# Moving one load within a period, and scaling the last outputs on one engine

## The chip, the cores and the metric

The kernel runs on one core of a Trainium2 chip. A core has five engines that run their own instruction streams and wait for each other by semaphores: TensorE (PE in the profile; its weight loads are listed apart as PEld), VectorE (DVE), ScalarE (ACT), GpSimd (POOL) and SyncE (SP), which here does nothing but issue DMAs. "SPq" and "ACTq" are the DMA-issuing queues of SyncE and ScalarE. The metric is the device time of one execution in microseconds (us); lower is better.

## The reference, cut to what matters

A gated linear attention over 4 batches, 8 heads, 768 tokens and 48 dimensions a head, followed by a two-layer block on the 3072 tokens (384 to 1024 to 384) with a SoLU activation and a layer norm between its two products:

```python
for t in range(S):                                   # S = 768
    state = alpha[:, :, t, :, None] * state + np.einsum('bhd,bhe->bhde', k[:, :, t], v[:, :, t])
    y[:, :, t] = np.einsum('bhd,bhde->bhe', q[:, :, t], state)
x = y.transpose(0, 2, 1, 3).reshape(B * S, H * D)    # (3072, 384)
h = x @ w_in                                         # (3072, 1024)
e = np.exp(h - h_max)
solu = h * e / (np.sum(e, axis=-1, keepdims=True) + 1e-09)
ln = (solu - mu) / np.sqrt(var + 1e-06) * g_ln
out = ln @ w_out                                     # (3072, 384)
```

`alpha`, the decay, is between 0.8 and 1.0.

## The kernel before

The 768 tokens are cut into G = 6 blocks of 128, and a block holds all four batches at once. For a block, attention is done in closed form: running products of alpha forwards and backwards (two families of scans on VectorE) scale the queries and keys, TensorE forms the scores, VectorE masks them, and TensorE reads out the old state (`read_state`) and the masked scores times v (`read_values`, 128 matmuls). The two-layer block follows: `up` makes 8 pieces of h (6 matmuls of 512 columns each) and their SoLU parts, `down` makes the output of one batch's 128 tokens in two halves (8 matmuls each), and `finish` scales it by the inverse deviation and stores it.

The work is overlapped by blocks. In period g (from 1 to 5) the up and down products of block g run in eight steps, and the attention of block g + 1 is woven into the same steps. The order is written out by hand: the instructions of each engine run in the order in which the code issues them, and no scheduler moves them. Two tables, `usual` and `first` (line 814 on), say what `attend` does in which step: `head` ahead of the step's up product, `behind` after it, `middle` and `tail` around the down product. `first` holds for period 1, `usual` for the others. Attention has nothing to do in period 5.

Three input buffers matter here, each with room for one block: `an` (alpha), `kn` and `qn`. They are filled by `load` (lines 137 to 143), which issues four DMAs of 192 KB from SyncE's queue, one for each batch. SyncE issues strictly in order, and a DMA waits there until its buffer has been read. For block a:

- "states v keys", step 0: the state is brought up to date, `load_v` fetches v, the keys are transposed and scaled, and k of block a + 1 is loaded.
- "on2 on0 on1", step 1: the forward scans.
- "lasts firsts", step 2: the queries are transposed and scaled, and q of block a + 1 is loaded.
- "alpha", step 6 (step 7 in period 1): `alpha_T` transposes alpha of block a + 1 out of `an` on VectorE, `alpha_over` tests its range on ScalarE (two passes over `an`), and `an` is loaded with alpha of block a + 2 if there is one.
- "back", step 7: the backward scans of block a + 1.

In steps 6 and 7 TensorE reads out the state and the values of block a. Alpha of blocks 0 to 3 is loaded by the opening code (line 800 for block 3); the step "alpha" loads blocks 4 (in period 1) and 5 (in period 2).

Stores also go through SyncE's queue, from the end of `finish` (line 534): a period has four of them. Behind the loop come the down products of the last block, all but their first half, and its four `finish` calls, which take another path (lines 510 to 517): the 128 x 384 result in PSUM is scaled by `r` into `o_sb` in two parts, columns 0 to 127 on VectorE and 128 to 383 on ScalarE, and stored from ScalarE's own queue.

Of the kernel before, what the change touches and what calls it, by code (L numbers as in the profile page):

```python
# [13 lines left out]
AF = mybir.ActivationFunctionType  # L14
ALU = mybir.AluOpType
AX = mybir.AxisListType
P = 128
# [15 lines left out]
def fast_path(ctx, tc, q, k, v, alpha, moe_w_in, moe_w_out, moe_g_ln, out):  # L33
# [12 lines left out]
    nc = tc.nc  # L46
    B, H, S, D = q.shape
    NTOK, DM = out.shape
    DFF = moe_w_in.shape[1]
    G = S // P  # L50
# [49 lines left out]
    an = const.tile([P, H, TQ, D], FP, name="an")  # L100
# [36 lines left out]
    def load(src, dst, g):  # L137
        t = slice(g * P, (g + 1) * P)
        for b in range(B):
            nc.sync.dma_start(  # L140
                out=dst[32 * b : 32 * b + 32].rearrange("t h u d -> t h (u d)"),
                in_=src[b, :, t, :].rearrange("h (t u) d -> t h (u d)", u=TQ),
            )
# [31 lines left out]
    def load_v(g):  # L175
        t = slice(g * P, (g + 1) * P)
        for dst, src in ((first_of, slice(0, E0)), (last_of, slice(E0, D))):
            for i in range(2):
                nc.sync.dma_start(
                    out=vn.rearrange("p b (h i) d -> p i (b h) d", i=2)[:, i, :, dst[i]],  # L180
                    in_=v[:, i::2, t, src].rearrange("b h p d -> p (b h) d"),
                )
# [11 lines left out]
    def firsts(src, dst):  # L194
        nc.vector.transpose(out=dst.rearrange("p h (t u) -> p h u t", u=TQ), in_=src[:, :, :, 0:E0])  # L195

    def lasts(src, dst):
        nc.vector.transpose(
            out=dst.rearrange("p j (i t u) -> p u j i t", u=TQ, i=2),
            in_=src[:, :, :, E0:D].rearrange("p (j i) u d -> p u j i d", i=2),  # L200
        )

    def alpha_T(g):
        nc.gpsimd.memset(aT[:, :, 0:1], 0.0)
        firsts(an, aT[:, 0:H, 1:SW])
        lasts(an, aT[:, H:NB, 1:SW])
# [20 lines left out]
    def scan_on(g, i):  # L227
        part = slice(NP * i, NP * i + NP)
        s = seed[i % 2]
        if i == 2:  # L230
            nc.vector.tensor_copy(out=fend[:, g], in_=h4[:, :, 1])

        least = small.tile([P, NP, 1], FP, name="least")
        nc.vector.tensor_scalar(out=least, in0=h4[:, part, 1:2], scalar1=LEAST, scalar2=None, op0=ALU.max)  # L234
        nc.vector.reciprocal(out=s[:, :, 0:1], in_=least)
        scan(aT[:, part], aT[:, part], s, False)

    def keys_T(g):
        firsts(kn, kT[:, 0:H])
        lasts(kn, kT[:, H:NB])  # L240

    def keys(g):
        for part in (slice(0, H), slice(H, NB)):
            nc.gpsimd.tensor_tensor(out=kT[:, part], in0=kT[:, part], in1=hk[:, part], op=ALU.mult)  # L244

    def apart():
        for i in range(2):
            nc.scalar.mul(
                out=qv[:, H : 2 * H].rearrange("p (j i) t -> p j i t", i=2)[:, :, i], in_=qe, mul=parity[:, i : i + 1]
            )  # L250

    def queries(i):
        part = slice(NP * i, NP * i + NP)
        q = qe if i == 2 else qv[:, part]
        nc.gpsimd.tensor_tensor(out=q, in0=q, in1=aT[:, part, 1:SW], op=ALU.mult)

    def decay(g):

        if g == 0:
            return  # L260
        for i in range(2):
            for rows, d in ((0, h4[:, i:H:2, 1:2]), (H, h4[:, H:NB, 1:2])):
                s = state[:, rows + i : rows + H : 2, all_of[i]]
                nc.gpsimd.tensor_tensor(out=s, in0=s, in1=d.to_broadcast([P, NP, D]), op=ALU.mult)
            nc.gpsimd.tensor_scalar(
                out=ends_state[:, :, i], in0=state[:, H + i : 2 * H : 2, last_of[i]], scalar1=parity[:, i : i + 1],
                scalar2=None, op0=ALU.mult,
            )
# [21 lines left out]
    def masked(half, batches=range(B)):  # L290
        a = masks[half]
        for b in batches:
            nc.vector.tensor_tensor(  # L293
                out=sT[:, b, half * NP : half * NP + NP], in0=a[b], in1=mask[:, None, :].to_broadcast([P, NP, P]),
                op=ALU.mult,
            )

    def keys_back(g, t=None):
        t = t or banks("tp", [NP, P], 3)
        for j in range(NB):  # L300
            nc.tensor.transpose(out=t[j // NP][:, j % NP], in_=kT[:, j], identity=ident)
        for i in range(3):
            nc.scalar.copy(out=kg[:, NP * i : NP * i + NP], in_=t[i])
# [201 lines left out]
    def finish(n):  # L505
        g, b = divmod(n, B)
        d = st[n]
        s, o = sums[:, n], d["o"][:, 0:DM]
        t0 = b * S + g * P
        if g == G - 1:  # L510
            o_sb = work.tile([P, DM], FP, name="o_sb")
            r = gr[g]["r"][:, b : b + 1]
            nc.vector.tensor_scalar(out=o_sb[:, 0:P], in0=o[:, 0:P], scalar1=r, scalar2=None, op0=ALU.mult)  # L513
            nc.scalar.activation(out=o_sb[:, P:DM], in_=o[:, P:DM], func=AF.Copy, scale=r)  # L514
            nc.scalar.dma_start(out=out[t0 : t0 + P, :], in_=o_sb)
            d.clear()
            return
        nc.vector.tensor_copy(out=s[:, 0:1], in_=d["o"][:, DM : DM + 1])
        t = small.tile([P, 1], FP, name="t")
        nc.vector.scalar_tensor_tensor(  # L520
            out=t, in0=s[:, 0:1], scalar=-1.0 / DFF, in1=s[:, 0:1], op0=ALU.mult, op1=ALU.mult
        )
        nc.vector.tensor_tensor(out=s[:, 3:4], in0=t, in1=gr[g]["s"][:, b : b + 1], op=ALU.add)  # L523
        if g == 0:

            o = work.tile([P, DM], FP, name="o_mean")
            nc.vector.scalar_tensor_tensor(
                out=o, in0=mean_sb, scalar=s[:, 0:1], in1=d["o"][:, 0:DM], op0=ALU.mult, op1=ALU.add
            )
        r = small.tile([P, 1], FP, name="r")  # L530
        nc.gpsimd.tensor_tensor(out=r, in0=s[:, 3:4], in1=mhalf, op=ALU.pow)  # L531
        o_sb = work.tile([P, DM], FP, name="o_sb")
        nc.scalar.activation(out=o_sb, in_=o, func=AF.Copy, scale=r)
        nc.sync.dma_start(out=out[t0 : t0 + P, :], in_=o_sb)
        d.clear()
# [154 lines left out]
    for i in (2, 0, 1):  # L690
        if i == 1:
# [3 lines left out]
            out=qe if i == 2 else qv[:, part], in0=t[i], in1=aT[:, part, 1:SW], op=ALU.mult  # L695
# [105 lines left out]
    for i in range(3):  # L801
# [11 lines left out]

    usual = dict(
        head={4: "keys_back", 5: "masked0", 6: "masked1"},
        behind={0: "states v keys", 1: "on2 on0 on1", 2: "lasts firsts", 3: "apart", 5: "decay", 6: "alpha", 7: "back"},
        tail={4: "scores0", 5: "scores1", 6: "begin read0 read1"},
        middle={7: "read2 read3 values"},
    )
# [2 lines left out]
        behind={0: "states v", 1: "on1", 2: "lasts firsts", 3: "apart", 5: "decay", 7: "alpha back"},  # L822
# [4 lines left out]
    def attend(a, what):  # L827

        more = a + 1 < G
        if what == "v":  # L830
            load_v(a)
        elif what == "keys":
            keys_T(a)
            keys(a)
            if more:
                load(k, kn, a + 1)
        elif what[:2] == "on":
            scan_on(a, int(what[2]))
        elif what == "lasts":
            lasts(qn, qe)  # L840
            queries(2)
        elif what == "firsts":
            firsts(qn, qv[:, 0:H])
            queries(0)
            queries(1)
            if more:
                load(q, qn, a + 1)
        elif what == "apart":
            apart()
        elif what == "decay":  # L850
            decay(a)
        elif what == "keys_back" and more:
            keys_back(a)
        elif what[:6] == "scores":
            scores(a, int(what[6]))
        elif what[:6] == "masked":
            masked(int(what[6]))
        elif what == "alpha" and more:
            alpha_T(a + 1)
            alpha_over(a + 1)  # L860
            if a + 2 < G:
                load(alpha, an, a + 2)
        elif what == "back" and more:
            for i in range(3):
                scan_back(a + 1, i)
        elif what == "begin":
            read_begin()
        elif what[:4] == "read":
            read_state(int(what[4]))
        elif what == "values":  # L870
            read_values(a)
        elif what == "states":
            next_state(a - 1)
# [57 lines left out]
    def compare(out, x, bound, op):  # L931
# [6 lines left out]
        out=chunks[:, :, 2], in0=sums[:, :, 2], scalar=0.25, in1=sums[:, :, 3], op0=ALU.mult, op1=ALU.is_le  # L938
# [6 lines left out]
    else:  # L945
# [9 lines left out]
        out=bad, in0=all_ok[0:1, 0:1], scalar1=float(P * ends[-1]), scalar2=None, op0=ALU.is_lt  # L955
# [451 lines left out]
```

## Time and profile before

| What | Value |
|---|---|
| Runs of the kernel before | 393.21, 398.35, 390.92, 398.58, 398.03 us |
| Their median | 398.03 us |
| The profiled execution | 393.18 us |
| Its span, from first to last instruction | 391.1 us |
| Mean granted clock of TensorE | 0.989 |
| Bytes moved by DMA | 30.79 MB |
| Alpha loads by `load` | 20 DMAs of 192 KB, 4.2 us to landing (median) |
| The two alpha loads of the step "alpha" | issued at 150.71 and 201.14 us |
| Stores of the last block | at 374.01, 376.56, 382.06 and 387.25 us |

The periods can be found in the trace by the first up product of each: period 1 starts at 112.5 us, period 2 at 153.6, period 3 at 212.2, period 4 at 269.3 and period 5 at 324.4. Busy time is a share of the span; a window's row gives its length, the busy time of each engine in it with the number of instructions, the granted clock of TensorE as a share of full speed, and the busy share of the DMA engines (which can come out a little over 1). In a timeline, the brackets at a line's end say how long the engine had been idle before it and what ended that.

### The profile page before, as it was taken

How to read it: one execution, taken by the hardware profiler on the slowest of the kernel's cores; microseconds unless marked ns; L12 is line 12 of the kernel's file. 1: busy time of each engine (PE TensorE's matmuls, PEld its weight loads, DVE VectorE, ACT ScalarE, POOL GpSimd, SP SyncE). 2: the span in 40 equal slices, each digit the busy share in tenths (PEclk: the TensorE clock that was granted, in tenths of full speed). 3: DMA queues.
4: the chain of work that ended last, by engine and by line, in shares of the span. 5: the costliest groups of instructions: out<-in, count | busy, mean ns of one | idle time of the engine just before them, and what ended most of it. 6: DMA issues, size and time to landing. Idle time of an engine off the chain costs nothing. (4 is left out here: it accounts for less than half of the span.)

```text
span 391.1 us, 10613 instructions
## 1 busy us (share of the span) xinstructions
PE 371.7 (95%) x4661; PEld 224.6 (57%) x4661; DVE 252.0 (64%) x421; ACT 143.6 (37%) x252; POOL 125.2 (32%) x135
## 2 busy tenths in 40 slices
PE   8798999788999999999998999999999999999995
PEld 8685345456665556656565656566555575555552
DVE  0989888996987767793754793755895511444420
ACT  2527774553424425225152225153223231333100
POOL 4020000041032992436412436412535620333210
PEclk9989999999899999999999999999999999999998
DMA  9975989303446303734030734000600000000011
GB/s 184 198 187 166 224 273 163 84 20 94 107 108 83 82 4 82 114 70 101 22 77 29 111 73 102 22 3 22 93 10 22 22 23 2 20 21 21 22 44 47
DMA packets 86567, 30.79 MB, mean 79 GB/s; under 512 B 68072, under 2 KB 84720, under 8 KB 86512
## 3 DMA queue, kind: packets, MB, share of 16 engines
q1 hardware_dynamic: 85488, 29.11, 34.8%
q10 hardware_dynamic: 1024, 0.92, 0.7%
q8 instruction: 38, 0.62, 0.7%
q14 instruction: 17, 0.14, 0.1%
HBM read 25.30 MB, written 4.72 MB: 77 GB/s over the span
## 5 line engine op out<-in xcount | busy, mean ns | idle before, releaser
L500 PE MATMUL o<-w_out,room 128*128 128x385 f32 x384 | 135.3, 496 | 1.1 <-DVE least L234 1.0
L389 PE MATMUL h<-x,w_in 128*128 128x512 f32 x288 | 132.2, 598 | 1.2 <-DVE g_col L619 1.2
L500 PEld LDWEIGHTS o<-w_out,room 128*128 128x128 f32 x384 | 72.0, 191 | 58.3 <-issue 15.9
L389 PEld LDWEIGHTS h<-x,w_in 128*128 128x128 f32 x288 | 53.0, 189 | 59.9 <-issue 48.7
L404 DVE TENSOR_TENSOR room<-h,e 128x512 f32<-128x512 f32 x40 | 27.7, 692 | 84.3 <-ACT e L403 84.1
L403 ACT ACTIVATE e<-h 128x512 f32<-128x512 f32 x40 | 23.9, 598 | 105.3 <-PE h L389 105.3
L531 POOL TENSOR_TENSOR r<-sums,mhalf 128x1 f32<-128x1 f32 x20 | 14.3, 715 | 138.7 <-DVE sums L523 138.7
L420 POOL TENSOR_TENSOR p<-p,e 128x512 f32<-128x512 f32 x30 | 41.7, 1390 | 15.7 <-ACT e L403 15.7
L405 ACT ACTIVATE u<-room 128x512 f32<-128x512 f32 x40 | 25.2, 631 | 42.3 <-DVE room L404 42.3
L293 DVE TENSOR_TENSOR sT<-a,mask 128x512 f32<-128x512 f32 x44 | 27.3, 682 | 9.9 <-PE a L282 9.9
L282 PE MATMUL a<-qv,kT 32*128 32x128 f32 x704 | 27.5, 288 | 4.5 <-DVE least L234 2.1
L282 PEld LDWEIGHTS a<-qv,kT 32*128 32x128 f32 x704 | 24.1, 194 | 12.0 <-issue 4.2
L220 DVE TENSOR_TENSOR_SCAN hT<-aT,unit 128x516 f32<-128x516 f32 x18 | 23.0, 1328 | 8.9 <-ACT aT L678 8.8
L244 POOL TENSOR_TENSOR kT<-kT,hT 128x1024 f32<-128x1024 f32 (+1 forms) x8 | 13.3, 1684 | 44.3 <-DVE kT L195 44.3
L420 DVE TENSOR_TENSOR p<-p,u 128x512 f32<-128x512 f32 x30 | 23.1, 771 | 6.5 <-ACT u L405 6.5
L314 PE MATMUL y<-sT,vn 128*32 128x128 f32 x768 | 23.6, 274 | 2.6 <-issue 2.0
L314 PEld LDWEIGHTS y<-sT,vn 128*32 128x32 f32 x768 | 20.9, 110 | 4.8 <-issue 3.9
L220 DVE TENSOR_TENSOR_SCAN aT<-aT,seed 128x516 f32<-128x516 f32 x18 | 23.0, 1278 | 0.6
L212 ACT ACTIVATE sq<-an,mone 128x1536 uint8<-128x1536 f32 x12 | 18.8, 1569 | 0.2
L314 PE MATMUL y<-qv,state 32*32 32x128 f32 x960 | 16.8, 277 | 1.0 <-DVE sT L293 0.9
L314 PEld LDWEIGHTS y<-qv,state 32*32 32x32 f32 x960 | 12.1, 103 | 7.8 <-issue 5.4
L351 ACT COPY x<-y 128x384 f32<-128x384 f32 x24 | 10.8, 481 | 15.5 <-PE y L314 15.4
(142 smaller groups left out, 379.4 us busy)
## 6 DMA issues: line engine op xcount, KB each, us to landing
an<-in_alpha_dram SPq DMA_DIRECT2D x20, 192.0 KB, 4.2
out_dram<-o_sb SPq DMA_DIRECT2D x20, 192.0 KB, 1.9
room<-in_moe_w_out_dram SPq DMA_DIRECT2D x8, 384.0 KB, 4.6
kn<-in_k_dram SPq DMA_DIRECT2D x16, 192.0 KB, 4.0
qn<-in_q_dram SPq DMA_DIRECT2D x16, 192.0 KB, 4.1
vn<-in_v_dram SPq DMA_DIRECT2D x10, 256.0 KB, 4.1
room<-in_moe_w_in_dram SPq DMA_DIRECT2D x16, 128.0 KB, 3.9
kn<-in_k_dram SPq DMA_DIRECT2D x4, 384.0 KB, 5.8
```

The costliest lines, as they stand in the source:

```text
L212: nc.scalar.activation(out=sq, in_=x, func=AF.Relu, scale=sign, bias=mone, accum_out=over[:, g, i : i + 1])
L220: nc.vector.tensor_tensor_scan(out=o, data0=a, data1=s, initial=1.0, op0=ALU.mult, op1=ALU.add)
L282: nc.tensor.matmul(a[b][:, i], lhsT=kT[quarter(b), kb], rhs=qv[quarter(b), qb], start=kb == h, stop=kb != h, tile_position=(32 * b, 0), sk ...
L293: nc.vector.tensor_tensor(out=sT[:, b, half * NP : half * NP + NP], in0=a[b], in1=mask[:, None, :].to_broadcast([P, NP, P]), op=ALU.mult,)
L314: nc.tensor.matmul(y_bank(b)[quarter(r), a], lhsT=lhsT, rhs=rhs, start=(b, r) not in begun, stop=stop, tile_position=(row, 32 * r), skip_g ...
L389: nc.tensor.matmul(h, lhsT=w_in[:, a, f * P : (f + 1) * P], rhs=d["x"][:, a].rearrange("p b t -> p (b t)"), start=(a == 0), stop=(a == KC ...
L403: nc.scalar.activation(out=e, in_=h, func=AF.Exp)
L404: nc.vector.tensor_tensor(out=u, in0=h, in1=e, op=ALU.mult)
L405: nc.scalar.activation(out=u2, in_=u, func=AF.Square)
L420: eng.tensor_tensor(out=p, in0=d[0][i] if f == 1 else p, in1=d[f][i], op=ALU.add)
L500: nc.tensor.matmul(d["o"][:, 0 : DM + 1], lhsT=u_of(g, f)[:, b * P : b * P + P], rhs=w_out[:, f], start=(f == 0), stop=(f == FC - 1), skip ...
L531: nc.gpsimd.tensor_tensor(out=r, in0=s[:, 3:4], in1=mhalf, op=ALU.pow)
```

## The change

Two edits. The load of the next alpha leaves the step "alpha" and becomes a step of its own, "load", in front of the forward scans of step 1 of the table `usual`. There it loads alpha of block a + 1, where the old place loaded that of block a + 2 one period earlier. The table `first` has no such step, so alpha of block 4 is loaded in period 2 and that of block 5 in period 3. In `finish`, the last block's scaling is one ScalarE instruction over all 384 columns.

```diff
         if g == G - 1:
             o_sb = work.tile([P, DM], FP, name="o_sb")
             r = gr[g]["r"][:, b : b + 1]
-            nc.vector.tensor_scalar(out=o_sb[:, 0:P], in0=o[:, 0:P], scalar1=r, scalar2=None, op0=ALU.mult)
-            nc.scalar.activation(out=o_sb[:, P:DM], in_=o[:, P:DM], func=AF.Copy, scale=r)
+            nc.scalar.activation(out=o_sb, in_=o, func=AF.Copy, scale=r)
             nc.scalar.dma_start(out=out[t0 : t0 + P, :], in_=o_sb)
...
     usual = dict(
         head={4: "keys_back", 5: "masked0", 6: "masked1"},
-        behind={0: "states v keys", 1: "on2 on0 on1", 2: "lasts firsts", 3: "apart", 5: "decay", 6: "alpha", 7: "back"},
+        behind={0: "states v keys", 1: "load on2 on0 on1", 2: "lasts firsts", 3: "apart", 5: "decay", 6: "alpha", 7: "back"},
...
         elif what == "alpha" and more:
             alpha_T(a + 1)
             alpha_over(a + 1)
-            if a + 2 < G:
-                load(alpha, an, a + 2)
+        elif what == "load" and more:
+            load(alpha, an, a + 1)
         elif what == "back" and more:
```

## The prediction

> **What bounds the kernel now.** I read the page's head first, then TensorE's waits, the order of time around the loads that move, the same passage of every period side by side, SyncE's queue, and the chain that ended last.
>
> The page:
> ```profile
> span 391.1 us, 10613 instructions
> PE 371.7 (95%) x4661; PEld 224.6 (57%) x4661; DVE 252.0 (64%) x421; ACT 143.6 (37%) x252; POOL 125.2 (32%) x135
> ```
> TensorE has work for 371.7 of 391.1 us. From about 110 us on its matmuls follow each other almost without a hole, so a change counts only if it takes time out of TensorE's row or out of the tail behind its last matmul. In TensorE's own waits (total, times, longest) the largest late item with no engine as its cause is:
> ```profile
> PE y L314 <- issue: 2.0, 2, 1.2
> ```
> "issue" means that no wait shown by the profile held it. The timeline places the longer one, in the second period:
> ```profile
> 201.14 1.82 SPq L140 DMA_DIRECT2D an<-in_alpha_dram  x4
> ...
> 204.31 2.81 PE L314 MATMUL y<-sT,vn 128*32 128x128 f32 x93
> ...
> 208.32 1.28 PE L314 MATMUL y<-sT,vn 128*32 128x128 f32 x35 [1.19 <-issue]
> ```
> An alpha load is issued at 201.14, and TensorE stops at 207.13 amid the 128 matmuls of read_values. The same 128 matmuls of every attention block, by windows (length, TensorE busy, granted clock, DMA share, GB/s):
> ```profile
> 104.92:109.77 4.85, 4.04 (x134) 1.00 0.64 135
> 146.69:150.85 4.16, 4.02 (x134) 1.00 0.02 4
> 204.31:209.53 5.22, 4.03 (x134) 1.00 0.38 98
> 262.99:266.62 3.63, 3.63 (x133) 1.00 0.06 20
> 318.11:321.74 3.63, 3.63 (x133) 1.00 0.16 59
> ```
> The clock is full in all five. The two dearest, 4.85 and 5.22 us, are the two with an alpha load in flight (issued at 103.13 and 201.14); without one it is 4.16 once and 3.63 twice.
>
> SyncE's queue between two periods:
> ```profile
> 158.27 4.59 SPq L179 DMA_DIRECT2D vn<-in_v_dram  x4
> 162.96 2.61 SPq L140 DMA_DIRECT2D kn<-in_k_dram  x4
> 166.73 0.37 SPq L534 DMA_DIRECT2D out_dram<-o_sb  x1
> 175.32 1.79 SPq L140 DMA_DIRECT2D qn<-in_q_dram  x4
> ```
> Last, the chain of waits at the end, and the nearest row for an undivided scaling, that of the earlier blocks (shortest, median and longest in ns):
> ```profile
> 386.37 0.35 DVE o_sb L513
> 386.72 0.02 issue
> 386.74 0.47 ACT o_sb L514
> ```
> ```profile
> L533 ACT ACTIVATE o_sb<-o,r x16: 580/580/582, 166.1 to 367.0; 128x384 f32<-128x384 f32 x16
> ```
> The two halves of the last scaling run one after the other: 0.35 + 0.02 + 0.47 = 0.84 us.
>
> **The change, part by part.** *The loads.* Neither bytes nor DMAs change. Alpha for block 3 still comes from line 800; those for blocks 4 and 5 (two loads of four DMAs) move. One was issued at 150.71, after period 1's reading; the other at 201.14, inside period 2's.
>
> The first is worth nothing where it was. The 7.29 us behind it (150.85 to 158.14) hold the same matmuls as 209.53 to 216.82 and 266.62 to 273.91, which have no load and also take 7.29 us. The second is worth what its passage costs over a clean one: 5.22 - 3.63 = 1.59 us. At the least, if the 4.16 us of period 1 is what such a passage costs anyway, it is 5.22 - 4.16 = 1.06 us. I take 1.59, since periods 3 and 4 both show 3.63.
>
> Why would a load stop TensorE without any wait? My reading is instruction supply. The page's queue table has 38 instruction packets of 0.62 MB on q8, some 16 KB each; 9322 TensorE instructions (4661 matmuls and as many weight loads) over 38 is about 245 to a packet, if that queue is TensorE's (an estimate). From 202.90 to 207.13 TensorE ran 190 matmuls and 189 weight loads, 379 instructions or one and a half packets, while the data engines were 0.68 busy. [...] I go with the rows: two of two passages with a load have a gap.
>
> At the new place, step 1 of the next period, each load stands in SyncE's queue behind v, k and the store at 166.73 (225.33 a period later), and ahead of the q load. It waits for nothing: the readers of the buffer, two transposes on VectorE and two range tests on ScalarE, ended by 150.7 and 201.1. Four issues take 1.8 us, so SyncE is free again at about 168.9, and q cannot be issued before 175.32 and 234.00 (it waits for VectorE's transposes of the old q). Even four issues at the longest seen for alpha, 1.84 us, end at 174.5. The store that stood behind the old load, at 206.92, followed its scaling at once and gains nothing. Alpha lands at worst 6.2 us after issue (its longest landing), near 175, and is read at 197.10: 22 us of cover. If that cover were gone, the transposes (2.09 + 1.11 us) and the three scans after them would be late and the next block's keys and scores with them. POOL issues no load.
>
> The collision at the new place: v and k hold the data engines at 1.0 to 1.2 from 160 to 168 and 0.59 from 168 to 170, so alpha lengthens a backlog of some 10 us by about 4. From 167.10 to 172.27 TensorE starts 15 matmuls and 14 weight loads, 29 instructions against the 379 after which it ran dry. I take 0. TensorE is unbroken there now, so nothing can be gained; the upper bound is 1.59 us for each of the two loads (the row of the old place).
>
> *The scaling.* Each of the four last chunks loses 0.35 us on VectorE and costs ScalarE 0.58 instead of 0.47. The first three lie beside TensorE, which is continuous from 370.12 to 386.26; they end about 0.26 us earlier or on time. The last one is the path: 0.84 becomes 0.58, so -0.26 us. ScalarE starts as promptly as VectorE: its Exp at 353.89 began 0.09 us after the matmul's end, VectorE's scaling at 386.36 0.10 after. Bounds: -0.26, and 0 if the wait costs ScalarE the rest.
>
> **The sum:** -1.59 - 0.26 = -1.85 us. The profiled execution took 393.18 us (span 391.1, 2.1 around it); with the change 391.3. The five runs lie in two groups, 390.92 and 393.21, and 398.03 to 398.58; the profiled execution belongs to the lower, the median, 398.03, to the upper. Nothing in one trace says what parts them, so I take the sum off the median: 396.2.
>
> **The rivals.**
> *Only the tail counts.* The gap is not the load's. [...] Then -0.26: 392.9 by the profiled execution, 397.8 by the median.
>
> *The upper group is the stall itself.* If in the longer runs such a passage stops TensorE by several microseconds more (the groups are about 5 us apart), then taking it away moves the runs to the lower group: 390.92 - 1.85 = 389.1 to 393.21 - 1.85 = 391.4. For it: nothing else late in TensorE's row is loose. Against: the opening has more waits, which stay, and has one such passage too (4.85 us).
>
> *Slower: TensorE runs dry at the new place.* v, k and alpha in one row starve the instruction supply in step 1 of both periods. Price: at most the 4.2 us of an alpha landing each, plus a clock that has to recover. The windows from 98 to 104 us show 0.76, 0.50 and 0.89 granted behind gaps of 1.48 and 0.85 us, and a down pass there took 4.55 instead of 2.86 us, 1.69 more. [...] 2 x (4.2 + 1.69) - 1.85 = +9.9 us: 408 by the median. It decides once TensorE needs more than it holds within the transfer; 29 instructions against 379 speak against it.
>
> That the change does something else than it says I leave at nothing: in either version there is one load for each block before its transposes.
>
> **How the numbers follow.** Forecast 0.52, tail only 0.22, upper group gone 0.18, dry at the new place 0.08. The predicted time is the forecast's, 396.2. The range goes from 389.0 (the third case's low end) to 399.0 (no gain, at the highest run shown). About 2% of 398, 8 us, is what a measurement of this kernel can tell from no change: faster means under 390.1, slower over 406.0. Faster is most of the lower half of the third case and a little for a gain that I don't see: 0.14; slower is the last case where it reaches its full price: 0.06; within, 0.80.
>
> **What would show it.** Right: the second period's passage takes 3.6 us with no issue gap, alpha is issued near 167 and 224 us with TensorE unbroken around both, and the chain ends in one ScalarE scaling of 0.58 us. Wrong: a gap in that passage with no load near it; issue gaps or a clock below 1.00 in the step behind the new loads; a q load later than its transposes; a transpose of alpha that waits for a DMA.

## The result, and the profile after

| | Before | After |
|---|---|---|
| Median of the runs | 394.80 us (79 runs) | 391.94 us (42 runs) |
| Lowest to highest | 390.65 to 399.87 us | 389.30 to 397.47 us |
| Profiled execution (its span) | 393.18 us (391.1) | 392.24 us (390.3) |

The time after is 0.9955 of the time before, with a 95% interval of 0.9937 to 0.9973: faster by about 1.8 us of 394.8 (1.1 to 2.5), within 2%. This ratio leaves out the runs that lie more than 1.5% above the fastest of the same kernel, at a lower granted clock, and so the gain by it is smaller than the difference of the medians of all runs, 2.9 us. The kernel before was run again beside the changed one, and its median over those 79 runs is 3.2 us below that of the five runs shown.

The passages of `read_values` (128 matmuls and 128 weight loads each) in the changed kernel, by windows (length, TensorE busy with its matmuls, granted clock, DMA share, GB/s). The first is the last one of the opening code, the others are those of periods 1 to 4:
```profile
104.85:109.89 5.04, 4.03 (x134) 1.00 0.60 135
146.86:151.48 4.62, 4.03 (x134) 1.00 0.03 7
204.94:209.09 4.15, 4.03 (x134) 1.00 0.14 51
262.48:266.11 3.63, 3.63 (x134) 1.00 0.06 21
317.60:321.23 3.63, 3.63 (x134) 1.00 0.17 59
```
The third line is the one that the change touches: 5.22 us before, 4.15 now, and its DMA share fell from 0.38 to 0.14. It is not clean, though: periods 3 and 4 need 3.63. A stop is still there, in the weight loads, with no load near it. Before:
```profile
204.31 2.55 PEld L314 LDWEIGHTS y<-sT,vn 128*32 128x32 f32 x93 [0.20 <-issue]
208.31 1.01 PEld L314 LDWEIGHTS y<-sT,vn 128*32 128x32 f32 x35 [1.46 <-issue]
```
and after, behind the same number of instructions and in the same 2.55 us:
```profile
204.94 2.55 PEld L314 LDWEIGHTS y<-sT,vn 128*32 128x32 f32 x93 [0.20 <-issue]
207.87 1.01 PEld L314 LDWEIGHTS y<-sT,vn 128*32 128x32 f32 x35 [0.39 <-issue]
```
The second window became longer (4.16 to 4.62), although nothing ahead of it was edited and hardly anything is transferred during it (0.03).

SyncE's queue after the change, around step 1 of periods 2 and 3:
```profile
167.36 0.37 SPq L533 DMA_DIRECT2D out_dram<-o_sb  x1
167.78 3.01 SPq L140 DMA_DIRECT2D an<-in_alpha_dram  x4
175.96 1.79 SPq L140 DMA_DIRECT2D qn<-in_q_dram  x4
...
225.30 1.97 SPq L140 DMA_DIRECT2D an<-in_alpha_dram  x4
233.50 1.79 SPq L140 DMA_DIRECT2D qn<-in_q_dram  x4
```
The alpha loads stand behind the store and ahead of q. Their issues took 3.01 and 1.97 us instead of the 1.8 that was reckoned with, but q is not held up: it waits for VectorE, as before (11.2 us in two waits of SyncE, against 16.3). Windows of one step's length from the issue of each load (the columns between the length and the clock are TensorE, its weight loads, VectorE, ScalarE and GpSimd) show TensorE unbroken at the new place, 5.17 of 5.17 us, with a DMA share of 0.92 and 1.07:
```profile
167.78:172.95 5.17, 5.17 (x15) 2.65 (x14) 5.03 (x9) 0.60 (x1) 1.00 (x1) 1.00 0.92 221
225.30:230.47 5.17, 5.17 (x15) 2.65 (x14) 5.03 (x8) 0.60 (x1) 1.03 (x1) 1.00 1.07 241
```
The end of the program in time:
```profile
385.79 0.58 ACT L513 ACTIVATE o_sb<-o,r 128x384 f32<-128x384 f32 x1 [4.61 <-PE o L500]
386.40 0.34 ACTq L514 DMA_DIRECT2D out_dram<-o_sb  x1
```
One scaling of 0.58 us stands where two took 0.84, and its wait is for the matmul alone. (Line 514 of the kernel before is 513 here.)

### The profile page after: what moved, and what is told of

The parts are those of the page before. It is cut to its first block, busy times and chain, and to the rows that moved or that the text cites. A ratio compares the mean times of both kernels' runs of the same rounds, so it can differ in the third digit from the quotient of the medians.

```text
span 390.3 us, 10598 instructions
## 1 busy us (share of the span) xinstructions
PE 371.2 (95%) x4661; PEld 224.1 (57%) x4661; DVE 250.6 (64%) x417; ACT 144.0 (37%) x252; POOL 125.2 (32%) x135
## 4 chain that ended last, share of the span: by engine, by line
PE 73%; DVE 13%; DMA 4%; ACT 4%; issue 2%; SPq 2%; ACTq 0%; DVEq 0%
PE o L500 30%; PE h L389 26%; PE y L314 9%; PE a L282 5%; DMA room<-in_v_dram 3%; SPq L152 2%; PE kv L364 2%; DMA room<-in_moe_w_in_dram 2%; DVE room L404 2%; DVE aT L220 1%; DVE top L597 1%; DVE low L605 1%; DVE sT L293 1%; DVE hT L220 1%; DVE top L594 1%
```

## The experiments

The theory: a transfer in the dense reading passage delays the fetch of TensorE's next instructions, and TensorE runs dry (it has started all the instructions that it holds and stands until more arrive). The main rivals: the gain comes from the scaling; period 2's passage is dear by its own work; writes into the on-chip memory hold TensorE's operands up.

A run of this kernel scatters by several microseconds, so each experiment is read first from the passages of its profiled execution and only then from its time.

**The moved load alone.** The kernel before with this:
```diff
-        behind={0: "states v keys", 1: "on2 on0 on1", ...
+        behind={0: "states v keys", 1: "load on2 on0 on1", ...
...
-            if a + 2 < G:
-                load(alpha, an, a + 2)
+        elif what == "load" and more:
+            load(alpha, an, a + 1)
```


> The kernel before with the moved load alone. Theory (a data transfer delays the fetch of TensorE's instructions, and TensorE runs dry in the dense reading passage): the passage of period 2 takes 4.15 us or less instead of 5.22, the tail keeps its two scalings in a row (0.84 us), and the ratio to before is 0.995 to 0.998. Rival (the gain comes from the scaling, or from elsewhere): the passage stays near 5.2 us or the ratio is 0.999 to 1.001.

Measured: 392.78 us median (22 runs), ratio 0.9983 (0.9952 to 1.0013). The passage of period 2:
```profile
206.06:210.15 4.09, 4.03 (x133) 1.00 0.16 56
```
and the end, still in two parts:
```profile
386.93 0.35 DVE L513 TENSOR_SCALAR o_sb<-o,r 128x128 f32<-128x128 f32 x1 [4.83 <-PEq L1375]
387.31 0.47 ACT L514 ACTIVATE o_sb<-o,r 128x256 f32<-128x256 f32 x1 [4.71 <-DVE o_sb L513]
```
The load alone takes 5.22 - 4.09 = 1.13 us out of the passage, as expected. Its ratio lies just above the expected band (0.995 to 0.998) and under the rival's (from 0.999), and the interval also holds 1: by the time alone nothing is decided.

**The undivided scaling alone.** The kernel before with the other edit:
```diff
-            nc.vector.tensor_scalar(out=o_sb[:, 0:P], in0=o[:, 0:P], scalar1=r, scalar2=None, op0=ALU.mult)
-            nc.scalar.activation(out=o_sb[:, P:DM], in_=o[:, P:DM], func=AF.Copy, scale=r)
+            nc.scalar.activation(out=o_sb, in_=o, func=AF.Copy, scale=r)
```


> The kernel before with the undivided scaling alone. Theory: the stretch from the last matmul to the last store shrinks by 0.26 us (0.84 to 0.58) and nothing else moves, so the ratio is 0.9993, which cannot be told from 1; the passage of period 2 stays at 5.0 to 5.3 us with its gap. Rival (the freed VectorE, or the checks that now run ahead of it, is where the gain is): a ratio of 0.997 or less.

Measured: 393.21 us median (20 runs), ratio 0.9969 (0.9942 to 0.9997). Period 2:
```profile
202.39:207.64 5.25, 4.03 (x134) 1.00 0.38 99
```
and the end:
```profile
384.39 0.58 ACT L513 ACTIVATE o_sb<-o,r 128x384 f32<-128x384 f32 x1 [4.61 <-PE o L500]
```
The passage keeps its gap and the end shrinks by the 0.26 us. The ratio is lower than expected and just inside the rival's band (0.997 or less), though the interval takes in 0.9993. So the two ratios cannot share out the gain by themselves, and I compared runs at one granted clock, 0.989 to 0.991, pooled over all experiments (means, with 1.96 standard errors):

| Kernel | Runs | Mean us |
|---|---|---|
| Before | 46 | 394.4 ± 0.3 |
| Scaling alone | 9 | 394.4 ± 0.9 |
| Load alone | 12 | 393.0 ± 0.6 |
| Both (the change) | 40 | 392.4 ± 0.4 |

There the load is worth 1.4 us, the scaling nothing that nine runs could show, and both together 2.0 ± 0.5. The profiles give less: 1.1 to 1.4 us for the passage (over all profiles with the load moved) and 0.26 for the end, 1.3 to 1.7 together, at the lower edge of this interval. The scaling's part rests on the rows at the end of the program alone.

**A needless load in period 3.** The changed kernel, and one more load at the old place in a period that had none. It fetches alpha of block 5 a second time, after its last use:
```diff
             alpha_over(a + 1)
+            if a + 2 == G:
+                load(alpha, an, a + 1)
```


> The changed kernel, plus one needless load of alpha of block 5 into the same buffer at the old place, in the step alpha of period 3, where no kernel had a load. Theory: the reading passage of period 3, 3.63 us until now, gets an issue gap and takes 4.7 to 5.3 us; the whole is about 1 us longer than the changed kernel (ratio to before 0.998). Rival (period 2's passage is dear for another reason, the load is not the cause): period 3 stays at 3.6 to 3.7 us without a gap.

Measured: 393.94 us median (11 runs), ratio 0.991 (0.9866 to 0.9954). The load was issued here:
```profile
260.14 1.82 SPq L140 DMA_DIRECT2D an<-in_alpha_dram  x4
```
and the passage of period 3:
```profile
263.32:267.70 4.38, 4.00 (x133) 1.00 0.46 124
```
It was 3.63 or 3.64 us in every profile without an added transfer there and with the program unshifted. With it, it is 4.38. The rival falls in the trace. The size, 0.75 us, is under the expected band (4.7 to 5.3 us), and the time speaks against a loss of 1 us: the expected ratio, 0.998, lies above the interval. With 11 runs that scatter by 9 us it is a weak witness, but it does not support the theory.

**Block 3's load moved too.** The changed kernel, and:
```diff
     alpha_over(2)
-    load(alpha, an, 3)
...
     first = dict(
-        behind={0: "states v", 1: "on1", ...
+        behind={0: "states v", 1: "load on1", ...
```


> The changed kernel, with the load of block 3's alpha moved as well: out of the opening code (where it is issued at 103 us, in front of the fifth reading passage, 5.04 us with a gap of 1.01) to step 1 of period 1. Theory: that passage falls to between 3.6 and 4.6 us, and the whole gains another 0.5 to 1.4 us on the changed kernel (ratio to before 0.992 to 0.994). Rival (the opening's gap has other causes): the passage stays at 4.8 to 5.1 us and the time is that of the changed kernel.

Measured: 392.14 us median (14 runs), ratio 0.9946 (0.9912 to 0.9979). The opening's last passage:
```profile
110.69:115.27 4.58, 4.03 (x133) 1.00 0.06 9
```
This is at the upper edge of what was expected, and 0.46 us less than in the changed kernel's first profile. It does not show that the load costs anything there: in the seven profiles that have this load in the opening code and the old start of the program, the same passage takes from 4.33 us (scaling alone) to 5.04 (the changed kernel's first), and 4.58 lies among them. What it shows is that 0.95 us over the clean 3.63 are there without any load (DMA share 0.06). The profiled execution was the longest of this kernel's runs, 397.26 us, though the passage itself ran at full clock. The time is that of the changed kernel within its interval, as the rival had it.

**Stores in place of the needless load.** The same number of bytes, out of the on-chip memory to a place in HBM that nothing reads (`spare`):
```diff
+    spare = nc.dram_tensor("spare_dram", (P, NB, P), FP, kind="Internal").ap()
...
             alpha_over(a + 1)
+            if a + 2 == G:
+                for b in range(B):
+                    nc.sync.dma_start(out=spare[32 * b : 32 * b + 32], in_=aT[32 * b : 32 * b + 32, :, 1:SW])
```


> The changed kernel, plus, in the step alpha of period 3, four stores of the transposed alpha (the same 768 KB in four DMAs) from the on-chip memory to a spare place in HBM. They use the same queue and data engines as the needless load of the run before, but write nothing on chip. Theory (the data engines are what the instruction fetch shares): the reading passage of period 3 gets a gap again and takes 4.1 to 5.0 us. Rival (writes into the on-chip memory hold up TensorE's operand reads): it stays at 3.63 us.

Measured: one run of 389.95 us, and in period 3:
```profile
259.64:263.65 4.01, 4.00 (x133) 1.00 0.41 120
```
It is 0.38 us dearer than the clean passage and just under the expected band. These transfers write nothing on chip, so such writes are not needed for the delay. Whether they add to that of the load, which was twice as dear, is read from the stops below.

**TensorE's program shifted.** The changed kernel with 92 more instructions before any work:
```diff
-    warm(18)
+    warm(9)
+    t = ps_o.tile([P, 512], FP, tag="o", name="warm")
+    for i in range(32):
+        nc.tensor.matmul(t[0:32, 0:32], lhsT=ones[:, 0:32], rhs=ones[:, 0:32], start=True, stop=True)
```


> The changed kernel with 92 more TensorE instructions in the warm-up at the start (9 of the 18 warm-up products, and 32 small ones of 32 by 32), which shift every border between two fetched pieces of TensorE's program by 92 of some 250 instructions and leave everything behind the start alone. Theory (what remains in periods 1 and 2 is a fetch that begins at an unlucky place in the dense stretch): the passages of periods 1 and 2, 4.62 and 4.14 us in the changed kernel, and the clean ones of periods 3 and 4 at 3.63 us, change places: at least one of the first two falls to 3.7 us or less, or one of the last two rises above 4.0. Rival (periods 1 and 2 are dearer by their own work): 4.1 to 4.7, 3.8 to 4.2, 3.63 and 3.63 us as before.

Measured: 392.20 us median (16 runs), ratio 0.9967 (0.9939 to 0.9995). The passages:
```profile
108.00:112.84 4.84, 4.03 (x134) 1.00 0.70 164
149.65:153.28 3.63, 3.63 (x134) 1.00 0.02 5
206.77:210.41 3.64, 3.64 (x134) 1.00 0.06 21
263.86:268.16 4.30, 3.84 (x133) 1.00 0.16 53
319.66:323.32 3.66, 3.66 (x132) 1.00 0.16 58
```
Periods 1 and 2 became clean, and period 3 became dear, with nothing changed in the passages but where in the program they stand. What remains in the changed kernel comes with the place, and not with the work.

**Where TensorE stops.** The weight loads of period 3 with the needless load, with the stores in its place, and in the shifted program:
```profile
263.32 3.43 PEld L314 LDWEIGHTS y<-sT,vn 128*32 128x32 f32 x127 [0.20 <-issue]
267.39 0.11 PEld L314 LDWEIGHTS y<-sT,vn 128*32 128x32 f32 x1 [0.65 <-issue]
...
259.64 3.42 PEld L314 LDWEIGHTS y<-sT,vn 128*32 128x32 f32 x127 [0.20 <-issue]
263.35 0.11 PEld L314 LDWEIGHTS y<-sT,vn 128*32 128x32 f32 x1 [0.28 <-issue]
...
263.86 2.12 PEld L314 LDWEIGHTS y<-sT,vn 128*32 128x32 f32 x80 [0.20 <-issue]
266.71 1.25 PEld L314 LDWEIGHTS y<-sT,vn 128*32 128x32 f32 x48 [0.73 <-issue]
```
The stop stands behind the same instruction with load and store. Under the shift it comes 47 weight loads earlier, which with their matmuls are about the 92 instructions that were put ahead. I counted all of TensorE's recorded instructions from the start of the program, in all ten profiles. Every stop over 0.25 us in these passages comes after instruction 3009 (opening), 4289 (period 1), 5825 (period 2) or 7361 (period 3), and the numbers are the same with and without the load, and in the shifted programs. They lie 1280, 1536 and 1536 apart, which are 5, 6 and 6 times 256. So TensorE stops at the borders of pieces of its program.

The fetches of these pieces have records too, of 16 KB each (queue q8 of the page: 38 packets, 0.62 MB). The table gives, for the fetch that starts in or just ahead of a passage, how many of TensorE's instructions had started by then, the border, how long TensorE stood there (by its weight loads), and when it went on, counted from the start of the fetch.

```
kernel               passage    fetch starts   by then   border   stood     went on   passage
before               period 2   205.61 us      5739      5825     1.46 us   2.70 us   5.22 us
after                period 2   205.26 us      5667      5825     0.39 us   2.61 us   4.15 us
after                period 1   146.86 us      4170      4289     0.85 us   2.53 us   4.62 us
after                period 3   263.00 us      7152      7361     0         -         3.63 us
needless load        period 3   264.78 us      7222      7361     0.65 us   2.61 us   4.38 us
stores in its place  period 3   260.85 us      7200      7361     0.28 us   2.50 us   4.01 us
program shifted      period 3   264.11 us      7221      7361     0.73 us   2.60 us   4.30 us
```
Over all stops of the ten profiles TensorE goes on 2.3 to 2.9 us after the start of the fetch. It stands when it reaches the border sooner than that, and the two causes of this can be told apart:

- *The place.* Without a load the fetch started 158 instructions ahead of the border in period 2, 119 in period 1 and 209 in period 3. Only the last was early enough.
- *The transfer.* In period 2 the same piece is fetched after 5659 to 5683 instructions in the six profiles with the load moved, and after 5739 and 5747 in the two with the load in its old place. In the kernel before, the fetch starts just when the load is nearly through: the data engines are 0.93 busy from 204.3 to 205.6 us and 0.06 busy with data in the 1.3 us after.

At TensorE's pace in the passage, 256 instructions in 3.63 us, the 72 instructions between the first two rows are 1.0 us, which is about the loss in period 2 (1.07). In period 3 the fetch came 70 and 48 instructions later, which are 1.0 and 0.7 us, and the losses were 0.75 and 0.38: some 0.3 us less, the time that the undisturbed fetch had to spare there. The store was cheaper than the load by 0.37 us: its fetch started 1.21 us into the passage instead of 1.46, and TensorE went on 2.50 us after that start instead of 2.61. Up to the stop TensorE kept its pace: 93 weight loads in 2.55 us with the load under way and without it, and 127 in 3.43 and 3.42 us with load and store. So writes on chip did not hold its operands up. By which means a transfer delays the start of a fetch, a shared queue or shared data engines, was not separated.

**Both cures together**, and the changed kernel again beside it:

> The changed kernel with both of the edits that took gaps away: block 3's alpha load moved to step 1 of period 1, and the 92 more instructions in the warm-up. Theory: the last passage of the opening code takes 3.6 to 4.6 us instead of 4.83, periods 1 and 2 stay at 3.63, period 3 at 4.3, period 4 at 3.7, so the whole is 0.5 to 1.5 us under the changed kernel in the same call (ratio to before 0.991 to 0.994). Rival (what one passage gains another gives back, or the opening hides it): the time is that of the changed kernel within 0.3 us.

> The changed kernel again, on the chip of the run beside it: a ratio to before of 0.995 to 0.996, as found already, passages of 4.2 to 4.6 us in periods 1 and 2 (the fetch alone) and 3.63 us in periods 3 and 4.

Measured: both cures 392.27 us median (22 runs), ratio 0.9986 (0.9955 to 1.0017); the changed kernel 392.63 (22 runs), ratio 0.9954 (0.992 to 0.9987). With both cures, the opening's last passage and period 3:
```profile
104.91:109.43 4.52, 4.03 (x134) 1.00 0.01 4
...
260.58:264.99 4.41, 4.00 (x133) 1.00 0.15 52
```
The passages did about as expected, but all five together take 4.52 + 3.63 + 3.63 + 4.41 + 3.84 = 20.03 us against 20.27 in the changed kernel's profile beside it (and 21.07 in its first): the shift only deals the delays out anew. The expected gain of 0.5 to 1.5 us did not come, and no version better than the changed kernel was found.

## Why the prediction was right, point by point

- *What bounds the kernel.* Right: time came out of one passage of TensorE (5.22 to 4.15 us) and out of the tail (0.84 to 0.58).
- *The first load is worth nothing.* Right as far as the trace goes: the stretch behind the old place had no loss to give back. Period 1's own passage lies between 4.15 and 4.62 us in the eight profiled executions with the old start of the program, load or no load behind it, and the 7.29 us behind it stayed 7.29.
- *The second load is worth 1.59 us.* The mechanism was right, the term too large. I measured against the clean 3.63 us and took 1.59 rather than the lower bound of 1.06. The trace shows 1.07. In the six profiles with the load moved and the old start of the program the passage takes 3.79 to 4.15 us, so the term is 1.07 to 1.43. What was missing is that TensorE stops at this border without a load too (0.39 us in the changed kernel), and that period 3 is clean only by where its border falls, as the shift showed (3.63 to 4.30 us). That the lower bound came so near is luck: period 1's 4.16 us belongs to another border, at another place in its passage.
- *Its own signs.* The passage of 3.6 us with no issue gap, named as the sign of being right, did not appear: 4.15 us, with a gap of 0.39 in the weight loads. The sign of being wrong, a gap with no load near it, did. The load was a cause of the gap and not the only one.
- *Where the supply of instructions shows.* In passages with no load near them TensorE stops in some and not in others: 4.62 us in period 1 and 4.15 in period 2 of the changed kernel, at DMA shares of 0.03 and 0.14, against 3.63 in periods 3 and 4, at 0.06 and 0.17. With 15 matmuls and 14 weight loads in 5.17 us, under 0.92 and 1.07, it did not stop.
- *The new place costs 0.* Right, by the two windows of 5.17 us under a DMA share of 0.92 and 1.07, as long as before (0.41 and 0.43).
- *The tail, -0.26 us.* Right: 0.84 to 0.58, in both kernels that have the edit.
- *The sum and the level.* By the trace, -1.07 - 0.26 = -1.33 us; the profiled spans differ by only 0.8, since the passages of the opening and of period 1 came out 0.19 and 0.46 longer in that execution. The ratio forecast, 391.33 to 393.18 or 0.9953, was met by 0.9955, partly by luck, for its load term was too large. The predicted 396.2 us is 4.3 above the median measured: I took the sum off a median of five runs, three of which were high, and that level did not hold. The range, down to 389.0, took it in. What parts the two groups goes with the granted clock: of the 116 runs of the kernel before that were taken beside the experiments, the 23 with a mean clock of 0.975 to 0.983 took 397.6 to 400.1 us, and the 17 with 0.994 or more 391.2 to 393.1.
- *The rivals.* "Tail only" fell with the load alone (5.22 to 4.09 us in the passage, the tail still in two parts). "The upper group is the stall" fell too: the changed kernel still has runs up to 398.55 us. "Dry at the new place" did not occur: the two windows there have TensorE busy throughout, at a clock of 1.00.

## What to carry to other kernels

Where a stretch of an engine's program consists of many short instructions (here 256 in 3.63 us), look at what is moved by DMA just then. A wait named "issue" in such a stretch, with no semaphore behind it, was here the program itself arriving late: 1.46 us at one border before the change, 0.39 after it. A load with slack may be tried where the engine runs long instructions; here, at 29 instructions in 5.17 us, a DMA share of 0.92 and 1.07 made nothing longer. And the repetitions of a passage in the same trace did not say by themselves what remains when a disturbance is gone, neither the cheapest (3.63 us) nor the dearest: each had the border of the fetched pieces at another place, 119, 158 and 209 instructions behind the start of the fetch in periods 1, 2 and 3. Look at which instruction the engine stops behind, and at when the fetch of the next piece starts.

## What the runs showed of the hardware that I had not expected

How much the start of this program decides in a passage some 150 and 260 us later: 92 instructions more at its head moved period 1's passage from 4.62 to 3.63 us and period 3's from 3.63 to 4.30.

And what much of the scatter is. The changed kernel's two profiles have spans of 390.3 and 388.2 us. The windows of the first, in the opening code:
```profile
98.00:100.00 2.00, 2.00 (x57) 0.59 0.15 30
100.00:102.00 2.00, 2.00 (x4) 0.56 0.26 98
```
and of the second:
```profile
98.00:100.00 2.00, 2.00 (x85) 1.00 0.40 78
100.00:102.00 2.00, 2.00 (x14) 1.00 0.26 98
```
In the first execution TensorE's clock was granted at 0.50 from 98.36 to 101.77 us, 3.41 us, behind two short stops of the opening; in the second it was 1.00 in both windows, and the same program ran 14 matmuls between 100 and 102 us instead of 4. The length of the stops does not tell the two apart: 1.47 and 0.85 us in the first, 1.48 and 0.86 in the second. Single runs of such a kernel have to be compared at the same granted clock. What decides whether the clock drops was not tried.
